# Routing by hand order: exponentials, gates and a cast moved by one step, running counts by TensorE

## The chip, the cores and the metric

The program runs on one core of one Trainium2 chip. The metric is the device time of one execution in microseconds (us); of several runs the median counts. A core has TensorE (PE, with PEld for its weight loads), VectorE (DVE), ScalarE (ACT), GpSimd (POOL), SyncE (SP) and 16 DMA engines. Each engine works through its own list in order; semaphores order the engines among each other.

## The reference

Three layers follow each other over 4608 tokens of 512 numbers: attention within chunks of 64 tokens, a mixture of eight experts with one expert per token, and a dense layer with a maximum over three products.

```python
# attention: 8 batches, 8 heads, 576 tokens in 9 chunks of 64, head size 64
scores = scale * q_c @ k_c.T; scores -= scores.max(-1)
attn = exp(scores); x = (attn / (attn.sum(-1) + 1e-9)) @ v_c
# experts
compute = x @ w_skip > 0                  # the others pass through
logits = x @ w_gate                       # 8 experts
e_idx = argmax(logits)                    # the first of equals
gate = (exp(logits - max) / (sum + 1e-9))[e_idx]
x[compute] += gate * (relu(x @ w1[e_idx]) @ w2[e_idx])
# dense
out = maximum(maximum(x @ m1, x @ m2), x @ m3) @ m_out
```

## The kernel before

The first stage is a software pipeline over 36 tiles of 128 tokens. Step t of its loop (`for t in range(NT + LAG)`) does the scores of tile t, the transposed exponentials of tile t-1 (`trp`), the values of tile t-2 (`xp`, scaled to `xg` by DVE and transposed on PE as `trx`) and the router's logits of tile t-3 (`lp`). Two tiles of tokens make a unit, whose q and k are turned by PE (`trq`, `trk`) one unit ahead. PE's list is in the program's order for the whole loop, the lists of DVE, ACT and POOL up to step 34 (`HAND`); after that a scheduler orders them, and SP's list, which issues the loads, is the scheduler's throughout.

Routing goes by groups of four tiles (the last two groups have two). When the logits of a group's last tile are there (steps 6, 10, 14, ... 30), `route` works out each token's expert: `mx`, `dl`, the exponentials `ex` on ACT (`rex`), the first largest `m8`, the sum `sm`, the gate's reciprocal into a column of the group's rows `xg`, the flag `comp`, and the one-hot row `oh` (`roh` in the trace). `route` is a generator: eight of its pieces (`BY = 8`) run at the end of that step, the others a step later, among them four additions that carry the running count per expert (`run`) from tile to tile. `store_x` sends the group's rows to DRAM by POOL's queue, behind the reciprocal. One step after `route` (7, 11, ... 31), `rank_of` lets PE add up the ranks in one PSUM tile (`rk`): one product of `upper_b` with the one-hot rows and one of `ones_b` with the four running counts. A group's rows lie in one of two buffers, so that group g+2 writes where group g was stored from.

```python
nc.tensor.matmul(rk, upper_b, oh[:, T], start=True, stop=False)                       # L420
link["rank", g] = nc.tensor.matmul(rk, ones_b, before[:, T], start=False, stop=True)  # L421
```

In the same loop expert 0's weights are loaded in eight pieces and split into two parts (`CUTS`, steps 13, 17, 19, 21, 25, 27, 29, 33): the cast `whi_e` on ACT (L93) at the end of the step, and right behind it the remainder `wlo_e` (L94), on POOL at steps 19 and 27 and on DVE otherwise. The router's weights `wcat` are loaded by SP (L607, L608) between the loads of units 2 and 3.

After the loop come the experts (their first products are `h`), and then the dense layer (`f_a`, `f_b`, `f_d`, `o`), whose text is not changed.

Of the kernel before, what the change touches and what calls it, by code (L numbers as in the profile page):

```python
# [34 lines left out]
COLS = NT  # L35
SLOTS = E * COLS
# [4 lines left out]
def kernel(  # L41
# [72 lines left out]
    ew = {}  # L114
# [7 lines left out]
    def expert_piece(e, i, pool, eng=None, raw=None):  # L122
        ew[e, i] = load_split(pool, *expert_src(e, i), eng, raw)
# [3 lines left out]
    kpool = p1.enter_context(tc.tile_pool(name="kpool", bufs=1))  # L127
# [5 lines left out]
    ones_b = kpool.tile([P, P], BF16, name="ones_b")  # L133
# [14 lines left out]
    prio = kpool.tile([P, GT, E], F32, name="prio")  # L148
# [4 lines left out]
    tok_f = kpool.tile([P, NT], F32, name="tok_f")  # L153
    col_i = kpool.tile([P, P], I32, name="col_i")
    col_f = kpool.tile([P, P], F32, name="col_f")
    run = [kpool.tile([P, GT, E], BF16, name=f"run{i}") for i in range(2)]
    nc.scalar.mul(run[0].rearrange("p t e -> p (t e)"), ones_b[:, :GT * E], 0.0)
    ids_sb = cpool.tile([P, SLOTS], I32, name="ids_sb")
    ids_0 = cpool.tile([P, 3], I32, name="ids_0")
    edge = kpool.tile([P, 2], I32, name="edge")  # L160
# [11 lines left out]
    apool = p1.enter_context(tc.tile_pool(name="apool", bufs=2))  # L172
# [182 lines left out]
    def route(g):  # L355
        (parts, lg), nt = groups[g], SIZES[g]
        T = slice(0, nt)

        def small(nm, dt=F32, w=None):
            return apool.tile([P, GT] if w is None else [P, GT, w], dt, tag=nm, name=f"{nm}_{g}", bufs=1)  # L360

        logit, skip = lg[:, T, :E], lg[:, T, E]
        mx = small("rmx")
        yield nc.vector.reduce_max(mx[:, T], logit, axis=AX)
        dl = small("rdl", w=E)
        yield nc.vector.tensor_tensor(dl[:, T], logit, mx[:, T].unsqueeze(2).to_broadcast([P, nt, E]), op=ALU.subtract)
        ex = small("rex", w=E)
        link["routed"] = nc.scalar.activation(ex[:, T], dl[:, T], AF.Exp)
        pr = small("rpr", w=E)
        yield nc.vector.scalar_tensor_tensor(pr[:, T], dl[:, T], 0.0, prio[:, T], op0=ALU.is_ge, op1=ALU.mult)  # L370
        m8 = small("rm8")
        yield nc.vector.reduce_max(m8[:, T], pr[:, T], axis=AX)
        sm = small("rsm")
        yield nc.vector.reduce_sum(sm[:, T], ex[:, T], axis=AX)
        yield nc.vector.tensor_scalar_add(sm[:, T], sm[:, T], 1e-9)
        for i, part in enumerate(parts):
            n = part.shape[1]
            yield nc.vector.reciprocal(part[:, :, DM], sm[:, i * n:i * n + n])
        store_x(g)
        comp = small("rcomp")  # L380
        yield nc.vector.tensor_single_scalar(comp[:, T], skip, 0.0, op=ALU.is_gt)
        m8c = small("rm8c")
        yield nc.vector.tensor_mul(m8c[:, T], m8[:, T], comp[:, T])
        oh = small("roh", BF16, w=E)
        yield nc.vector.tensor_tensor(oh[:, T], prio[:, T], m8c[:, T].unsqueeze(2).to_broadcast([P, nt, E]), op=ALU.is_equal)
        before, after = run[g % 2], run[(g + 1) % 2]
        for j in range(nt):
            last = j == nt - 1
            yield nc.vector.tensor_tensor(
                after[:, 0, :] if last else before[:, j + 1, :], before[:, j, :], oh[:, j, :], op=ALU.add)  # L390
        eo = small("reo")
        yield nc.vector.tensor_scalar(eo[:, T], m8[:, T], float(-COLS), float(E * COLS + P * SLOTS), op0=ALU.mult, op1=ALU.add)
        nc.vector.scalar_tensor_tensor(eo[:, T], comp[:, T], float(-P * SLOTS), eo[:, T], op0=ALU.mult, op1=ALU.add)
        picks[g] = oh, eo

    def advance(gen, by):
        for _ in range(by):
            if next(gen, None) is None:
                return

    def fill_first(have):
        cp = ps_sm("pad_ps")[:, :1]
        nc.tensor.matmul(cp, ones_b, have, start=True, stop=True)
        pad = apool.tile([P, 1], I32, name="pad", bufs=1)
        nc.vector.scalar_tensor_tensor(pad, cp, -1.0, edge[:, 0:1], op0=ALU.mult, op1=ALU.add)
        nc.vector.tensor_tensor(pad, pad, edge[:, 1:2], op=ALU.max)
        nc.vector.tensor_single_scalar(pad, pad, 7, op=ALU.arith_shift_right)
        nc.vector.tensor_tensor(have, have, pad, op=ALU.add)

    def count_first():  # L410
        cp = ps_sm("first_ps")[:, :1]
        nc.tensor.matmul(cp, ones_b, run[0][:, 0, E - 1:E], start=True, stop=True)
        nc.vector.tensor_scalar_add(cnt_i[:, 2 * E:], cp[0:1, :], float(P))

    def rank_of(g):
        oh = picks[g][0]
        before = run[g % 2]
        T, nt = slice(0, SIZES[g]), SIZES[g]
        rk = ps_sm(f"rk{g}")[:, :nt * E].rearrange("p (t e) -> p t e", e=E)
        nc.tensor.matmul(rk, upper_b, oh[:, T], start=True, stop=False)  # L420
        link["rank", g] = nc.tensor.matmul(rk, ones_b, before[:, T], start=False, stop=True)  # L421
        picks["rk", g] = rk

    def rank_out(g):
# [176 lines left out]
    def in_turn(load, *what):  # L601
        with tc.issue_after(link["load"].ins) if "load" in link else nullcontext():
            load(*what)

    first_v = {1: (0, 1), 2: (2, 3), 3: (4, 5), 4: (6, 7)}
    def load_gates():
        nc.sync.dma_start(wcat[:, :, :E], w_gate.rearrange("(c p) e -> p c e", p=P))  # L607
        link["load"] = nc.sync.dma_start(wcat[:, :, E], w_skip.rearrange("(c p) -> p c", p=P))  # L608

    for u in range(5):  # L610
        in_turn(load_qk, u)
        for part in first_v.get(u, ()):
            in_turn(load_v, part)
        if u == 2:
            in_turn(load_gates)
        if u < 2:
            pair_heads(u, 0)
            pair_heads(u, 1)
            if u == 0:
                qk_transpose(0, 0)  # L620
                qk_transpose(0, 1)
    LAG, late, raws_0 = GT + 5, range(NT - 2), {}
    HAND = NT - 2
    CUTS = [13, 17, 19, 21, 25, 27, 29, 33]
    ASIDE = (19, 27)
    BY = 8
    routing = {}
    fetch = None
    in_order = ExitStack()
# [5 lines left out]
    def last_of(t):  # L635
        if 0 <= t < NT:
            g, j = PLACE[t]
            if j + 1 == SIZES[g]:
                return g
        return None  # L640

    for t in range(NT + LAG):
        u, s = divmod(t, 2)
        hand = t < HAND
# [38 lines left out]
            qk_transpose(u + 1, s, "k")  # L683
        if t < NT:
            exponentials(t)
        if 0 <= t - 2 < NT:
            x_transpose(t - 2)
            x_out(t - 2)
        if t < NT:
            cross_up(t)  # L690
        g = last_of(t - 3)
        if g is not None:
            routing[g] = route(g)
            advance(routing[g], BY if hand else 99)
        g = last_of(t - 4)
        if g is not None:
            advance(routing[g], 99)
            rank_of(g)
            if not t + 1 < HAND:
                rank_out(g)  # L700
        g = ranked if hand else last_of(t - 4)
        if g is not None:
            if g == 2:
                count_first()
            place(g)
            if g == FIRST or START[g] + SIZES[g] == DIRECT:
                for i in range(max(late[0], t - LAG + hand), START[g + 1]):
                    send_id(i)
                late = range(START[g + 1], NT - 2)
            if START[g] + SIZES[g] == DIRECT:  # L710
                load_ids(ids_0[:, 2:], ids_rows[:, 2:3])
            if g == FIRST:
                fill_first(run[(g + 1) % 2][:, 0, 0:1])
                load_ids(ids_0[:, :2], ids_rows[:, :2])
                xgs[0] = [four_kb([P, XW], F32, f"xg_0_{j}") for j in range(2)]
                rows = START[g + 1] * P
                fetch = t + 3
        if t in CUTS:
# [500 lines left out]
```

## Time and profile before

| | |
|---|---|
| runs shown | 1122.0 us median of 3 (1117.78, 1122.0, 1122.71) |
| profiled execution | 1125.63 us; span from first to last instruction 1123.9 us |
| TensorE's granted clock, mean over the span | 0.954 |
| busy | PE 1035.0 us (92%), DVE 577.0 (51%), ACT 432.9 (39%), POOL 356.4 (32%) |
| first stage | span up to about 215 us; the first product of expert 0 starts at 223.9 us |

A row of the timeline has the start and the length in us, engine, line, operation, what it writes and reads, and in brackets how long the engine stood idle before it and who released it. Views by tile list the engine's idle time before the tile's instructions, in us and times. Views of windows give busy time and number of instructions per engine, the granted clock (1.00 is full, 0.50 half), the DMA engines' share and GB/s.

### The profile page before, as it was taken

The numbers are of one execution on the slowest core, as the hardware profiler recorded it, in microseconds if no ns is written. First come the engines' busy times: TensorE is split into PE (matmuls) and PEld (weight loads), VectorE is DVE, ScalarE is ACT, GpSimd is POOL, SyncE is SP. The second block draws the span as 40 slices with busy tenths as digits, with TensorE's granted clock in tenths as the row PEclk, the third lists the DMA queues.
The fourth block names the chain that finished last, engine by engine and source line by source line (L and its number), as shares of the span: only waits on it lengthen the run. The fifth ranks groups of instructions, "written<-read, shape, count | busy, mean of one in ns | idle before, by whom it ended". The sixth has DMA issues, their size and how long they took to land.

```text
span 1123.9 us, 19739 instructions
## 1 busy us (share of the span) xinstructions
PE 1035.0 (92%) x7544; PEld 881.6 (78%) x7544; DVE 577.0 (51%) x1116; ACT 432.9 (39%) x771; POOL 356.4 (32%) x379
## 2 busy tenths in 40 slices
PE   7987888897899998999899799999999999999996
PEld 6876777785788887787687688888887888788995
DVE  4566654547873657551479871335234342443241
ACT  5665565433442434441344342222322232223231
POOL 3534554354441335340333141222311140113011
PEclk9898888698999998999999999999999999999998
DMA  9999572246783737471998924664466545666681
GB/s 220 272 271 299 154 196 86 79 153 218 255 285 112 237 109 264 165 229 58 311 298 294 330 87 151 199 193 122 160 193 181 170 140 166 183 185 208 195 263 38
DMA packets 213042, 217.14 MB, mean 193 GB/s; under 512 B 48203, under 2 KB 177227, under 8 KB 212928
## 3 DMA queue, kind: packets, MB, share of 16 engines
q1 hardware_dynamic: 199744, 174.18, 52.0%
q0 software_dynamic: 10592, 33.20, 8.4%
q10 hardware_dynamic: 2592, 8.26, 2.1%
q8 instruction: 70, 1.15, 0.4%
q14 instruction: 44, 0.36, 0.1%
HBM read 175.15 MB, written 41.83 MB: 193 GB/s over the span
## 4 chain that ended last, share of the span: by engine, by line
PE 42%; DMA 5%; issue 3%; POOL 1%; DVE 1%; SPq 0%; ACT 0%; POOLq 0%; DVEq 0%; ACTq 0%
PE f_a L774 5%; PE f_a L775 5%; PE f_a L776 5%; PE o L774 4%; PE o L775 4%; PE o L776 4%; DMA ws<-m_sums 3%; PE f_d L774 3%; PE f_d L776 3%; PE f_d L775 3%; DMA m_sums<-n_q 1%; PE f_b L774 1%; PE f_b L776 1%; PE f_b L775 1%; PE trf L948 1%
## 5 line engine op out<-in xcount | busy, mean ns | idle before, releaser
L94 POOL TENSOR_TENSOR fh<-best,fh 128x512 fp32r<-128x512 f32 (+1 forms) x60 | 76.3, 1278 | 371.9 <-ACT fh L93 286.2
L774 PE MATMUL f_a<-x_t,ws 128*128 128x512 f32 (+1 forms) x270 | 100.3, 372 | 1.0 <-DVE best L1102 1.0
L775 PE MATMUL f_a<-x_t,ws 128*128 128x512 f32 (+1 forms) x270 | 99.7, 369 | 0.0
L776 PE MATMUL f_a<-x_t,ws 128*128 128x512 f32 (+1 forms) x270 | 99.5, 369 | 0.0
L93 ACT CAST whi_e<-raw_e 128x1024 fp32r<-128x1024 f32 x64 | 66.1, 1050 | 59.5 <-DMA raw_e<-in_moe_w_dram 29.8
L774 PE MATMUL h<-xhi,whi_e 128*128 128x256 f32 x256 | 75.6, 296 | 11.9 <-ACT whi_e L93 5.4
L775 PE MATMUL o<-wlo_m,fh 128*128 128x512 f32 x216 | 84.5, 391 | 0.0
L774 PE MATMUL o<-whi_m,fh 128*128 128x512 f32 x216 | 84.2, 392 | 0.0
L776 PE MATMUL o<-whi_m,fh 128*128 128x512 f32 x216 | 83.4, 393 | 0.0
L94 POOL TENSOR_TENSOR wlo_e<-raw_e,whi_e 128x1024 fp32r<-128x1024 f32 x23 | 58.3, 2540 | 53.9 <-ACT whi_e L93 52.6
L775 PE MATMUL h<-xlo,whi_e 128*128 128x256 f32 x256 | 74.7, 292 | 0.1
L776 PE MATMUL y<-whi_e,hlo 128*128 128x512 f32 x184 | 73.0, 400 | 1.7 <-DVE hlo L781 1.4
L774 PE MATMUL y<-whi_e,hhi 128*128 128x512 f32 x184 | 73.9, 403 | 0.6 <-ACT hhi L841 0.6
L776 PE MATMUL h<-xhi,wlo_e 128*128 128x256 f32 x256 | 74.2, 291 | 0.0
L775 PE MATMUL y<-wlo_e,hhi 128*128 128x512 f32 x184 | 72.5, 396 | 0.0
L93 ACT CAST fh<-best 128x512 fp32r<-128x512 f32 (+1 forms) x60 | 34.6, 579 | 94.1 <-DVE best L1104 56.3
L94 DVE TENSOR_TENSOR wlo_e<-raw_e,whi_e 128x1024 fp32r<-128x1024 f32 x41 | 50.8, 1256 | 35.9 <-ACT whi_e L93 34.0
L774 PEld LDWEIGHTS h<-xhi,whi_e 128*128 128x128 f32 x256 | 51.3, 200 | 14.9 <-issue 6.0
L774 PEld LDWEIGHTS f_a<-x_t,ws 128*128 128x128 f32 x270 | 51.1, 189 | 10.1 <-DVE best L1102 1.5
L776 PEld LDWEIGHTS f_a<-x_t,ws 128*128 128x128 f32 x270 | 51.1, 189 | 8.6
L775 PEld LDWEIGHTS f_a<-x_t,ws 128*128 128x128 f32 x270 | 51.1, 189 | 8.4
L765 POOL DMA_INDIRECT x_dram<-xg,ids_sb x20 | 20.5, 1026 | 115.7 <-DVEq L989 46.7
(222 smaller groups left out, 2692.2 us busy)
## 6 DMA issues: line engine op xcount, KB each, us to landing
ws<-m_sums SPq DMA_DIRECT2D x135, 512.0 KB
raw_e<-in_moe_w_dram SPq DMA_DIRECT2D x64, 512.0 KB
ws<-m_sums SPq DMA_DIRECT2D x45, 256.0 KB
x<-x_dram SPq DMA_DIRECT2D x36, 256.0 KB
x_dram<-xg POOLq DMA_DIRECT2D x8, 1040.0 KB
v_all<-in_v_dram SPq DMA_DIRECT2D x32, 256.0 KB
out_dram<-os SPq DMA_DIRECT2D x32, 256.0 KB
m_sums<-n_raw ACTq DMA_DIRECT2D x18, 448.0 KB
```

The costliest lines, as they stand in the source:

```text
L93: nc.scalar.copy(hi, src),
L94: eng.tensor_tensor(lo, src, hi.bitcast(F32), op=ALU.subtract),
L765: ins = nc.gpsimd.indirect_dma_start(out=x_dram[:, :], out_offset=bass.IndirectOffsetOnAxis(ap=ids, axis=0), in_=xg, in_offset=None, bound ...
L774: nc.tensor.matmul(acc, ahi, bhi, start=first, stop=False, skip_group_check=onto)
L775: nc.tensor.matmul(acc, ahi, blo, start=False, stop=False, skip_group_check=onto)
L776: return nc.tensor.matmul(acc, alo, bhi, start=False, stop=last, skip_group_check=onto)
L948: nc.tensor.transpose(tr[:, i * P:(i + 1) * P], row[:, c * P:(c + 1) * P], ident)
```

## The change

- `route` is no longer a generator. In its step it now runs ahead of the transposition `trx` in the program, and it goes as far as `oh`. What is left (the sum, the gate's reciprocal, `eo`, the store, the count) is a new function `gates`, one step later. So ACT's exponentials `rex` have a step until DVE reads them, and the store's issue on POOL stands a step later.
- The running count is kept per group: DVE sums the four one-hot rows (`rgot`) and adds them once. The ranks within a group are added by PE: three more products of `ones_b` with one-hot rows (one in a group of two).
- `CUTS` is one lower, so that load and cast come a step earlier; the remainder stays at the old step.
- `wcat` is loaded by POOL's queue, ahead of its first other transfers.

```diff
         link["routed"] = nc.scalar.activation(ex[:, T], dl[:, T], AF.Exp)
+        comp = small("rcomp")
+        nc.vector.tensor_single_scalar(comp[:, T], skip, 0.0, op=ALU.is_gt)
...
+        m8c = small("rm8c")
+        nc.vector.tensor_mul(m8c[:, T], m8[:, T], comp[:, T])
+        oh = small("roh", BF16, w=E)
+        nc.vector.tensor_tensor(oh[:, T], prio[:, T], m8c[:, T].unsqueeze(2).to_broadcast([P, nt, E]), op=ALU.is_equal)
...
+    def gates(g):
...
+        nc.vector.reduce_sum(sm[:, T], ex[:, T], axis=AX)
+        nc.vector.tensor_scalar(eo[:, T], m8[:, T], float(-COLS), float(E * COLS + P * SLOTS), op0=ALU.mult, op1=ALU.add)
+        nc.vector.tensor_scalar_add(sm[:, T], sm[:, T], 1e-9)
+        nc.vector.scalar_tensor_tensor(eo[:, T], comp[:, T], float(-P * SLOTS), eo[:, T], op0=ALU.mult, op1=ALU.add)
...
+            nc.vector.reciprocal(part[:, :, DM], sm[:, i * n:i * n + n])
         store_x(g)
...
-        for j in range(nt):
-            last = j == nt - 1
-            yield nc.vector.tensor_tensor(
-                after[:, 0, :] if last else before[:, j + 1, :], before[:, j, :], oh[:, j, :], op=ALU.add)
+        nc.vector.reduce_sum(got, oh[:, T].rearrange("p t e -> p e t"), axis=AX)
+        nc.vector.tensor_tensor(after, before, got, op=ALU.add)
...
-        link["rank", g] = nc.tensor.matmul(rk, ones_b, before[:, T], start=False, stop=True)
+        for j in range(nt - 1):
+            nc.tensor.matmul(
+                rk[:, j + 1:], ones_b, oh[:, j:j + 1].to_broadcast([P, nt - 1 - j, E]), start=False, stop=False)
+        link["rank", g] = nc.tensor.matmul(
+            rk, ones_b, before.unsqueeze(1).to_broadcast([P, nt, E]), start=False, stop=True)
...
-        nc.sync.dma_start(wcat[:, :, :E], w_gate.rearrange("(c p) e -> p c e", p=P))
-        link["load"] = nc.sync.dma_start(wcat[:, :, E], w_skip.rearrange("(c p) -> p c", p=P))
+        nc.gpsimd.dma_start(wcat[:, :, :E], w_gate.rearrange("(c p) e -> p c e", p=P))
+        nc.gpsimd.dma_start(wcat[:, :, E], w_skip.rearrange("(c p) -> p c", p=P))
...
-    CUTS = [13, 17, 19, 21, 25, 27, 29, 33]
-    ASIDE = (19, 27)
+    CUTS = [12, 16, 18, 20, 24, 26, 28, 32]
+    ASIDE = (18, 26)
...
+        g = last_of(t - 3)
+        if g is not None and hand:
+            route(g)
         if 0 <= t - 2 < NT:
             x_transpose(t - 2)
...
-            routing[g] = route(g)
-            advance(routing[g], BY if hand else 99)
+        if g is not None and not hand:
+            route(g)
+            gates(g)
         g = last_of(t - 4)
         if g is not None:
-            advance(routing[g], 99)
+            if t <= HAND:
+                gates(g)
             rank_of(g)
...
         if t in CUTS:
             i = CUTS.index(t)
-            expert_piece(0, i, wpool, nc.gpsimd if t in ASIDE else None, raw=raws_0[i])
...
+            nc.scalar.copy(hi_0, raws_0[i])
+            ew[0, i] = hi_0, lo_0
+        if t - 1 in CUTS:
+            i = CUTS.index(t - 1)
+            hi_0, lo_0 = ew[0, i]
+            (nc.gpsimd if t - 1 in ASIDE else nc.vector).tensor_tensor(lo_0, raws_0[i], hi_0.bitcast(F32), op=ALU.subtract)
```

On DVE, at the first group's ranks (step 7), between the shift of the scores (`ex`, from `sc`) and the scaling of the next tile (`sm`), there stood before:

```order
L275 TENSOR_TENSOR ex_825<-sc_806,mx_823 128x2x4x64
L383 TENSOR_TENSOR rm8c_861<-rm_0_769,rcomp_776 128x4
L385 TENSOR_TENSOR roh_863<-prio,rm8c_861 128x32
L389 TENSOR_TENSOR run_114<-run_114,roh_863 128x8 x3
L389 TENSOR_TENSOR run_115<-run_114,roh_863 128x8
L392 TENSOR_SCALAR reo_869<-rm_0_769 128x4
L393 SCALAR_TENSOR_TENSOR reo_869<-rcomp_776,reo_869 128x4
L427 TENSOR_TENSOR rrs_875<-rk_872,roh_863 128x32
L322 TENSOR_SCALAR sm_907<-xp_890 128x8
```

and in the changed kernel, at the same place:

```order
L275 TENSOR_TENSOR ex_827<-sc_808,mx_825 128x2x4x64
L389 TENSOR_REDUCE rsm_863<-rex_757 128x4
L390 TENSOR_SCALAR reo_769<-rm_0_763 128x4
L391 TENSOR_SCALAR rsm_863<-rsm_863 128x4
L392 SCALAR_TENSOR_TENSOR reo_769<-rcomp_759,reo_769 128x4
L395 RECIPROCAL xg_356<-rsm_863 128x4
L399 TENSOR_REDUCE rgot_870<-roh_767 128x8
L400 TENSOR_TENSOR run_115<-run_114,rgot_870 128x8
L432 TENSOR_TENSOR rrs_879<-rk_873,roh_767 128x32
L322 TENSOR_SCALAR sm_911<-xp_894 128x8
```

The one-hot rows `roh`, which PE's ranks read, have left this step; the sum, the reciprocal and the one addition of the count have come in.

On ACT, around the first piece of expert 0's weights (steps 12 and 13), a step running from `aT` to `vm`, there stood before:

```order
L229 COPY vm_1288<-v_all_134 64x260
L292 COPY aT_1442<-trp_1437 128x512
L251 COPY qT_1346<-trq_1_1444 128x2x2x128
L353 COPY lg_1098<-lp_1450 128x9
L251 COPY kT_1359<-trk_1_1456 128x2x2x128
L282 ACTIVATE ex_1435<-ex_1435 128x512
L342 COPY xt_1468<-trx_1463 128x512
L229 COPY vm_1388<-v_all_135 64x260
L93 CAST whi_e_0_1471<-raw_e_0_912 128x1024
L292 COPY aT_1541<-trp_1536 128x512
```

and in the changed kernel:

```order
L229 COPY vm_1294<-v_all_134 64x260
L729 CAST whi_e_0_1389<-raw_e_0_806 128x1024
L292 COPY aT_1451<-trp_1446 128x512
L251 COPY qT_1350<-trq_1_1453 128x2x2x128
L353 COPY lg_1100<-lp_1459 128x9
L251 COPY kT_1363<-trk_1_1465 128x2x2x128
L282 ACTIVATE ex_1444<-ex_1444 128x512
L342 COPY xt_1477<-trx_1472 128x512
L229 COPY vm_1395<-v_all_135 64x260
L292 COPY aT_1545<-trp_1540 128x512
```

The cast has moved ahead by one step of ACT's list, while DVE's remainder `wlo_e` stands behind the same shift of the scores as before.

## Rows read from the trace of the kernel before

**Rows 1.** The page's part 2: TensorE's granted clock in 40 equal slices, tenths.

```profile
PEclk9898888698999998999999999999999999999998
```

**Rows 2.** DVE's line of each step's maxima: ns least/median/most, first and last start.

```profile
L273 DVE TENSOR_REDUCE mx<-sc x36: 679/680/691, 12.1 to 211.6; 128x8 f32<-128x512 f32 x36
```

**Rows 3.** Timeline of PE, two steps next to each other, the scores' first row.

```profile
51.11 0.65 PE L264 MATMUL sc<-kT,qT 64*64 64x64 f32 x32
...
54.95 0.65 PE L264 MATMUL sc<-kT,qT 64*64 64x64 f32 x32
```

**Rows 4.** By tile, `rk`: PE's idle time until a releaser, us, times.

```profile
  DVE run L389: 6.9, 7
  DVE roh L385: 4.8, 5
  ACT ex L282: 2.4, 2
```

**Rows 5.** By tile, `trx`: the same.

```profile
  DVE xg L324: 13.3, 11
```

**Rows 6.** Timeline around one group's ranks, DVE, POOL and PE.

```profile
111.63 0.39 DVE L385 TENSOR_TENSOR roh<-prio,rm8c 128x32 bf16<-128x32 f32 x1
...
112.03 0.61 POOL L235 COPY qr<-qt 128x512 f32<-128x512 f32 x1
112.05 1.55 DVE L389 TENSOR_TENSOR run<-run,roh 128x8 bf16<-128x8 bf16 x4
...
112.08 0.19 PE L420 MATMUL rk<-roh,upper_b 128*128 128x32 bf16 x1 [1.10 <-DVE roh L385]
...
113.46 0.18 PE L421 MATMUL rk<-run,ones_b 128*128 128x32 bf16 x1 [1.19 <-DVE run L389]
```

**Rows 7.** Timeline around one piece of expert 0's weights.

```profile
125.87 1.04 ACT L93 CAST whi_e<-raw_e 128x1024 fp32r<-128x1024 f32 x1
...
126.95 1.22 DVE L94 TENSOR_TENSOR wlo_e<-raw_e,whi_e 128x1024 fp32r<-128x1024 f32 x1 [3.48 <-ACT whi_e L93]
...
128.58 0.69 DVE L324 TENSOR_TENSOR xg<-xp,sm 128x512 f32<-128x512 f32 x1
...
129.41 0.63 PE L337 MATMUL trx<-ident,xg 128*128 128x128 f32 x4 [1.96 <-DVE xg L324]
```

**Rows 8.** Windows: length, busy (x) of PE, PEld, DVE, ACT, POOL, PEclk, DMA share, GB/s.

```profile
28.00:206.00 178.00, 145.37 (x2656) 131.17 (x2655) 104.67 (x314) 110.66 (x227) 87.13 (x140) 0.87 0.75 202
206.00:227.00 21.00, 19.65 (x204) 17.99 (x204) 13.54 (x65) 6.62 (x16) 6.50 (x7) 0.52 0.29 104
20.00:106.00 86.00, 72.47 (x1415) 66.34 (x1409) 51.75 (x149) 56.38 (x118) 40.16 (x72) 0.88 1.06 275
```

**Rows 9.** Timeline of ACT in the first of the two steps of rows 3.

```profile
54.10 0.64 ACT L251 COPY kT<-trk 128x512 f32<-128x512 f32 x1 [0.32 <-PE trk L249]
```

**Rows 10.** Timeline of PE: two rank products of which the second waits for nothing.

```profile
213.77 0.18 PE L420 MATMUL rk<-roh,upper_b 128*128 128x32 bf16 x1 [0.64 <-ACT lg L353]
213.80 0.19 PE L421 MATMUL rk<-run,ones_b 128*128 128x32 bf16 x1
```

**Rows 11.** Timeline: the sum in routing on DVE, and POOL's store with a later write.

```profile
108.52 0.19 DVE L374 TENSOR_REDUCE rsm<-rex 128x4 f32<-128x32 f32 x1 [1.10 <-ACT rex L368]
...
187.06 0.81 POOL L496 DMA_DIRECT2D x_dram<-xg  x1 [9.01 <-DVE sm L322]
...
191.93 0.15 POOL L320 MEMSET xg<- 128x14 f32 x2 [2.35 <-DMA x_dram<-xg]
```

**Rows 12.** Timeline of SP: the first of the two loads of `wcat`.

```profile
15.44 1.53 SPq L607 DMA_DIRECT2D wcat<-in_moe_w_gate_dram  x1
```

**Rows 13.** Waits of PE, 0 to 60 us and 160 to 215 us: total, times, longest.

```profile
PE trp L289 <- issue: 1.8, 1, 1.8
...
PE sc L264 <- issue: 3.9, 8, 1.3
```

**Rows 14.** DVE's line of the running count: ns least/median/most.

```profile
L389 DVE TENSOR_TENSOR run<-run,roh x36: 130/164/603, 44.3 to 231.3; 128x8 bf16<-128x8 bf16 x36
```

More of the change, by code (lines that the diff above doesn't have):

```diff
@@ L155 @@
     col_f = kpool.tile([P, P], F32, name="col_f")
-    run = [kpool.tile([P, GT, E], BF16, name=f"run{i}") for i in range(2)]
-    nc.scalar.mul(run[0].rearrange("p t e -> p (t e)"), ones_b[:, :GT * E], 0.0)
+    run = [kpool.tile([P, E], BF16, name=f"run{i}") for i in range(2)]
+    nc.scalar.mul(run[0], ones_b[:, :E], 0.0)
     ids_sb = cpool.tile([P, SLOTS], I32, name="ids_sb")
@@ L363, in route @@
         mx = small("rmx")
-        yield nc.vector.reduce_max(mx[:, T], logit, axis=AX)
+        nc.vector.reduce_max(mx[:, T], logit, axis=AX)
         dl = small("rdl", w=E)
-        yield nc.vector.tensor_tensor(dl[:, T], logit, mx[:, T].unsqueeze(2).to_broadcast([P, nt, E]), op=ALU.subtract)
+        nc.vector.tensor_tensor(dl[:, T], logit, mx[:, T].unsqueeze(2).to_broadcast([P, nt, E]), op=ALU.subtract)
         ex = small("rex", w=E)
         link["routed"] = nc.scalar.activation(ex[:, T], dl[:, T], AF.Exp)
+        comp = small("rcomp")
@@ L369, in route @@
+        nc.vector.tensor_single_scalar(comp[:, T], skip, 0.0, op=ALU.is_gt)
         pr = small("rpr", w=E)
-        yield nc.vector.scalar_tensor_tensor(pr[:, T], dl[:, T], 0.0, prio[:, T], op0=ALU.is_ge, op1=ALU.mult)
+        nc.vector.scalar_tensor_tensor(pr[:, T], dl[:, T], 0.0, prio[:, T], op0=ALU.is_ge, op1=ALU.mult)
         m8 = small("rm8")
-        yield nc.vector.reduce_max(m8[:, T], pr[:, T], axis=AX)
-        sm = small("rsm")
-        yield nc.vector.reduce_sum(sm[:, T], ex[:, T], axis=AX)
@@ L375, in route @@
-        yield nc.vector.tensor_scalar_add(sm[:, T], sm[:, T], 1e-9)
+        nc.vector.reduce_max(m8[:, T], pr[:, T], axis=AX)
+        m8c = small("rm8c")
+        nc.vector.tensor_mul(m8c[:, T], m8[:, T], comp[:, T])
+        oh = small("roh", BF16, w=E)
+        nc.vector.tensor_tensor(oh[:, T], prio[:, T], m8c[:, T].unsqueeze(2).to_broadcast([P, nt, E]), op=ALU.is_equal)
+        eo = small("reo")
+        picks[g] = oh, eo
+        routing[g] = ex, m8, comp
+    def gates(g):
+        parts, nt = groups[g][0], SIZES[g]
+        T = slice(0, nt)
+        ex, m8, comp = routing[g]
+        oh, eo = picks[g]
+        sm = apool.tile([P, GT], F32, tag="rsm", name=f"rsm_{g}", bufs=1)
+        nc.vector.reduce_sum(sm[:, T], ex[:, T], axis=AX)
+        nc.vector.tensor_scalar(eo[:, T], m8[:, T], float(-COLS), float(E * COLS + P * SLOTS), op0=ALU.mult, op1=ALU.add)
+        nc.vector.tensor_scalar_add(sm[:, T], sm[:, T], 1e-9)
+        nc.vector.scalar_tensor_tensor(eo[:, T], comp[:, T], float(-P * SLOTS), eo[:, T], op0=ALU.mult, op1=ALU.add)
@@ L376, in route @@
         for i, part in enumerate(parts):
             n = part.shape[1]
-            yield nc.vector.reciprocal(part[:, :, DM], sm[:, i * n:i * n + n])
+            nc.vector.reciprocal(part[:, :, DM], sm[:, i * n:i * n + n])
         store_x(g)
[L380 to L385, printed above, removed]
@@ L386, in route @@
-        before, after = run[g % 2], run[(g + 1) % 2]
-        for j in range(nt):
-            last = j == nt - 1
-            yield nc.vector.tensor_tensor(
-                after[:, 0, :] if last else before[:, j + 1, :], before[:, j, :], oh[:, j, :], op=ALU.add)
-        eo = small("reo")
-        yield nc.vector.tensor_scalar(eo[:, T], m8[:, T], float(-COLS), float(E * COLS + P * SLOTS), op0=ALU.mult, op1=ALU.add)
-        nc.vector.scalar_tensor_tensor(eo[:, T], comp[:, T], float(-P * SLOTS), eo[:, T], op0=ALU.mult, op1=ALU.add)
@@ L394, in route @@
[L394 to L399, printed above, removed]
+        before, after = run[g % 2], run[(g + 1) % 2]
+        got = apool.tile([P, E], F32, tag="rgot", name=f"rgot_{g}", bufs=1)
+        nc.vector.reduce_sum(got, oh[:, T].rearrange("p t e -> p e t"), axis=AX)
+        nc.vector.tensor_tensor(after, before, got, op=ALU.add)
     def fill_first(have):
@@ L411, in count_first @@
         cp = ps_sm("first_ps")[:, :1]
-        nc.tensor.matmul(cp, ones_b, run[0][:, 0, E - 1:E], start=True, stop=True)
+        nc.tensor.matmul(cp, ones_b, run[0][:, E - 1:E], start=True, stop=True)
         nc.vector.tensor_scalar_add(cnt_i[:, 2 * E:], cp[0:1, :], float(P))
@@ L614 @@
         if u == 2:
-            in_turn(load_gates)
+            load_gates()
         if u < 2:
@@ L623 @@
     HAND = NT - 2
-    CUTS = [13, 17, 19, 21, 25, 27, 29, 33]
-    ASIDE = (19, 27)
-    BY = 8
+    CUTS = [12, 16, 18, 20, 24, 26, 28, 32]
+    ASIDE = (18, 26)
     routing = {}
@@ L690 @@
             cross_up(t)
-        g = last_of(t - 3)
-        if g is not None:
-            routing[g] = route(g)
-            advance(routing[g], BY if hand else 99)
+        if g is not None and not hand:
+            route(g)
+            gates(g)
         g = last_of(t - 4)
         if g is not None:
-            advance(routing[g], 99)
+            if t <= HAND:
+                gates(g)
             rank_of(g)
@@ L712 @@
             if g == FIRST:
-                fill_first(run[(g + 1) % 2][:, 0, 0:1])
+                fill_first(run[(g + 1) % 2][:, 0:1])
                 load_ids(ids_0[:, :2], ids_rows[:, :2])
@@ L719 @@
             i = CUTS.index(t)
-            expert_piece(0, i, wpool, nc.gpsimd if t in ASIDE else None, raw=raws_0[i])
+            hi_0 = wpool.tile([P, 1024], F32R, tag="w", name=f"whi_e0_{i}")
+            lo_0 = wpool.tile([P, 1024], F32R, tag="w", name=f"wlo_e0_{i}")
+            nc.scalar.copy(hi_0, raws_0[i])
[4 more added lines that the diff above has]
+            (nc.gpsimd if t - 1 in ASIDE else nc.vector).tensor_tensor(lo_0, raws_0[i], hi_0.bitcast(F32), op=ALU.subtract)
+            ew[0, i] = [w.rearrange("p (a b) -> p a b", a=2) if i > 3 else w for w in ew[0, i]]
         if t == fetch:
@@ L730 @@
     cp = ps_sm("cnt_ps")[:, :E]
-    nc.tensor.matmul(cp, ones_b, run[len(SIZES) % 2][:, 0, :], start=True, stop=True)
+    nc.tensor.matmul(cp, ones_b, run[len(SIZES) % 2], start=True, stop=True)
     nc.vector.tensor_copy(cnt_i[:, :E], cp[0:1, :])
```

## The prediction, on record before the changed kernel ran

> **What bounds the kernel now.** I began with the page's slices of the granted clock [rows 1]: in the whole span the low digits lie in the first fifth, one slice at 6. The change touches that part alone, the 36 steps of attention and routing. Next I looked for the stage's beat. DVE's maxima come once a step, 36 times from 12.1 to 211.6 us [rows 2]: 199.5 us in 35 intervals, 5.70 us a step. The PE timeline shows what a step costs when nothing waits: from one step's scores to the next's 3.84 us [rows 3], with PE's work back to back. 35 such intervals would take 134.4 us, so the stage loses 65 us. The rest of this working asks where they are, by the views of the tiles for which PE waits, and then by windows for the clock.
>
> PE waits in two places. Ahead of the rank products it stands 6.9 us for the running count, 4.8 for the one-hot rows and 2.4 where the page names ACT [rows 4]: 14.1 us in the seven groups ranked inside the hand order. Ahead of `trx` it stands 13.3 us for the scaled rows, 11 times [rows 5]. The timelines show why. At the ranks, the one-hot rows are made after the shift of the same step's scores and then come four dependent additions, 1.55 us; PE stands 1.10 us for the first and 1.19 for the second [rows 6]. At a piece of weights, DVE holds its list 3.48 us for ACT's cast, which is ACT's last work of the step; the scaling queued behind comes late, and PE stands 1.96 us [rows 7]. PE's list cannot pass a waiting product, so these 27.4 us lie on the path.
>
> After such stops the granted clock falls. From 28 to 206 us its mean is 0.87 [rows 8]; it has only a full and a half level (2.4 and 1.2 GHz), so 0.13 x 178 = 23.1 us of full-speed work were lost. 14.1 + 13.3 + 23.1 = 50.5 us of the 65; most of the rest are stops marked "issue", 1.8 and 3.9 us in the two places shown [rows 13], which the change doesn't address.
>
> **The change part by part.** All sums go from the profiled execution, 1125.6 us (span 1123.9 and 1.7 around it); the median of the runs is 1122.0, 3.6 less, and I subtract the same amount from it.
>
> *Ranks.* The one-hot rows are now ready a step ahead, the count of the groups before likewise; no operand of the rank products is made in their own step any more. -14.1 us. Later in that step is then only PE itself: 21 more products with their weight loads in the hand order (3 for each of 7 groups). Two rank products that waited for nothing start 0.03 us apart and run 0.19 [rows 10]: between 0.6 (21 x 0.03) and 4.0 us (21 x 0.19); I take 0.1 each, since the weights are loaded anew each time, +2.1.
>
> *Casts.* The remainder stays at its step and the cast stands a step ahead, so the 3.48 us waits of DVE go. The exponentials' sum moves a step too: DVE's 1.10 us for `rex` [rows 11] goes, which also delayed the scaling. -13.3. What is late next is ACT: in a quiet step it idles just 0.32 us [rows 9] against a cast of 1.04 [rows 7], 0.72 us over for each of 8 pieces. The casts are there before as well, so the price lies between 0 and 5.8 us; I take the middle, +3.
>
> *Clock.* Some dips follow the "issue" stops and will stay. Bounds are 0 and 23.1 us; I take about half, -12. The scheduled tail from 206 to 227 us runs at 0.52 [rows 8] and loses 0.48 x 21 = 10.1 us; a stop for a cast precedes it, but there PE also meets routing's last chains. Bounds 0 and 10.1, I take -3.
>
> *Router's weights.* SP is rid of two issues, the first of 1.53 us [rows 12], 3.1 for two like it, just ahead of the loads of unit 3, behind which PE stops 1.8 us [rows 13]. On POOL they stand before its first copies, where it waits for loads anyway; the packets then mix with the very first q and k. Between -3.1 and +3.1; I take half of the gain, -1.5. The Trainium skill (DMA: Bandwidth & Descriptors, Issuing engines are not separate DMA queues) says that all queues share the same 16 DMA engines, so that another issuer saves its issue time alone. The DMA share of 1.06 from 20 to 106 us [rows 8] agrees that those engines are full there; by this rule the term would be nearer 0, and the time 1.5 us longer.
>
> *Store.* The store's issue on POOL stands a step later, behind the reciprocal in `gates`; queued behind it are the next step's index writes and copies of q and k, which have steps to spare (POOL waited 9.01 us to issue the store shown [rows 11]). But the buffer is written again by group g+2, now three steps after the issue, not four. Once in the trace POOL stands 2.35 us for a store, and goes on at 191.93, 4.87 us after that store's issue at 187.06 [rows 11]. Three quiet steps are 11.5 us. Between 0 and 7 x 2.35 = 16.5 us; I take +1.5, near 0, as the space is twice the one landing seen.
>
> *DVE's load.* Eight operations after the shift become seven in the rank step, and eight seven in the step before, each about 0.2 us in a gap that DVE has there; it is busy 104.7 of 178 us [rows 8]. I count 0. The running count took from 0.13 to 0.60 us [rows 14], the long ones beside POOL's copies [rows 6]. Were six operations with two operands in each group (four before the one-hot rows, two in `gates`) held 0.44 us (0.60 - 0.16), 7 groups would cost 18 us of DVE, and the time would be 1103 if all of it reached PE. The Trainium skill (SBUF — State Buffer, SBUF: two separate sides) gives a lock as the reason: a VectorE operation with two operands in SBUF and one of GpSimd exclude each other for the whole instruction. That rule speaks against the four such operations that now stand together; rows 14 agree with it in the range, and rows 6 in the neighbour.
>
> Sum: -14.1 - 13.3 - 12 - 3 - 1.5 + 2.1 + 3 + 1.5 = -37.3. 1125.6 - 37.3 = 1088.3; by the median 1122.0 - 37.3 = 1084.7, so **1085 us**. What follows the stage starts earlier by the same and is otherwise the same text; the scheduler changes some order in the dense layer, for which I count 0.
>
> **Rivals.**
> - *All the clock returns.* With no stop left above a microsecond, the other 11.1 of the stage and 7.1 of the tail come too: 1085 - 18 = 1067. For it: quiet steps run at full clock. Against: the "issue" stops.
> - *The clock stays down.* The waits go, but short ones remain in each cast and rank step and the dips with them: 12 + 3 back, 1100.
> - *Loads bind.* From 20 to 106 us the DMA engines are full at 275 GB/s [rows 8]. By 206 us 43.7 MB pass at most (36.0 from 28 us on at 202 GB/s, 7.7 before at 275). At 275 that takes 159 us, no bound; at 238, halfway between the two rates, 184, so the stage could gain 22 us; with the 6.6 us added, 15: 1107.
> - *DVE binds*, by operations held 18 us beside POOL's: 1103. For it: the range of rows 14. Against: DVE is free two fifths of the stage.
> - *Given back at the seam*, where expert 0 waits for the ids, the gather and the next weights, whatever the stage does: 1120.
> - *Slower, by the store.* A store lands so late that group g+2's scaling waits on DVE and PE behind it, and half a dip follows. Before any loss, 37.3 us must be eaten, 5.6 more to be measured: 6.1 us in each of 7 groups. That is a landing some 18 us after issue (11.5 + 6.1). At 7.5 us each: 1122 + 15 = 1137. For it: full DMA engines early on. Against: the one wait seen ends within 5 us.
>
> **How the numbers follow.** Forecast 0.42, with its own range 1077 to 1094; all the clock 0.13; clock down 0.14; loads 0.12; DVE 0.07; seam 0.05; slower 0.07. The bounds of the terms alone reach from 1122 - 27.4 - 33.2 - 3.1 + 0.6 = 1059 to 1122 - 27.4 + 3.1 + 4.0 + 5.8 + 16.5 = 1124. The range 1066 to 1112 leaves out the seam, the slower case and the ends. A measurement of this kernel tells about 0.5% (5.6 us) from no change: faster 0.88, same 0.05, slower 0.07.
>
> **What would show it.** In the changed profile: no idle time of PE before `rk` released by `roh` or `run`; idle time before `trx` by `xg` under 4 us; DVE not waiting for `whi_e` or `rex` in the hand order; the last of the 36 maxima near 176 us (211.6 less 36); a granted clock of 0.93 or more from 28 us to the end of the steps. POOL or DVE released by `x_dram<-xg` more than once would be the store's price. The prediction is wrong if the beat stays above 5 us with those waits gone, or if the first product of expert 0 comes less than 20 us earlier than 223.9.

## The result, and the profile after

The changed kernel takes 1089.7 us (1087.7 to 1093.9) where the kernel before, run beside it, takes 1120.4: a ratio of 0.973 (95% interval 0.969 to 0.977), 30.8 us less. Forecast were 1085, in a range from 1066 to 1112. The profiled execution has a span of 1092.1 us.

The whole gain lies ahead of expert 0. Its first product starts at 191.8 us instead of 223.9, 32.0 earlier; from there to the end of the span it is 900.3 us, before 900.0. The page's slices of the clock and of the DMA share:

```profile
PEclk9989978989999989998999899999999999999998
DMA  9999684467738185428998545663566546666581
```

Against [rows 1] no slice of the first fifth is under 7. The maxima of the steps, then what PE waits for ahead of `rk` and of `trx` (each by tile: total, times), answering to [rows 2, 4, 5]:

```profile
L273 DVE TENSOR_REDUCE mx<-sc x36: 679/680/692, 12.1 to 179.5; 128x8 f32<-128x512 f32 x36
...
L423 PE MATMUL rk<-roh,ones_b x26: 166/169/182, 39.8 to 199.6; 128*128 128x8 bf16 x10, 128*128 128x24 bf16 x8, 128*128 128x16 bf16 x8
...
  ACT lg L353: 1.3, 1
...
  ACT aT L292: 42.9, 12
  PE lp L348: 0.7, 1
  DVE xg L324: 0.6, 1
```

The last maxima come 32 us earlier; the beat is 4.78 us (167.4 in 35), not 5.70. No rank product waits for DVE any more: the 1.3 us for `lg` belong to a group that is ranked after the last step's scores, at 181.65 us. The scaled rows cost 0.6 us instead of 13.3. But `trx` has a new releaser, ACT's copy `aT`; the tile view adds PE and its weight loads. The waits from 28 to 185 us keep them apart (total, times, longest):

```profile
POOL vm L223 <- DMA v_all<-in_v_dram: 23.4, 6, 9.7
...
PE trx L337 <- ACT aT L292: 20.6, 5, 7.0
...
DVE wlo_e L734 <- ACT whi_e L729: 15.3, 3, 6.7
ACT whi_e L729 <- DMA raw_e<-in_moe_w_dram: 14.3, 4, 5.7
...
ACT vm L229 <- DMA v_all<-in_v_dram: 6.4, 3, 5.3
...
POOL xg L320 <- DMA x_dram<-xg: 4.2, 1, 4.2
```

Two loads are late: expert 0's raw weights and `v`. The second longest stop stands at step 13; here are its rows on SyncE's queue, ACT and PE:

```profile
58.31 2.60 SPq L100 DMA_DIRECT2D raw_e<-in_moe_w_dram  x1
...
60.75 0.41 ACT L229 COPY vm<-v_all 64x260 f32<-64x260 f32 x1
66.88 1.04 ACT L729 CAST whi_e<-raw_e 128x1024 fp32r<-128x1024 f32 x1 [5.73 <-DMA raw_e<-in_moe_w_dram]
67.83 0.58 ACT L292 COPY aT<-trp 128x512 f32<-128x512 f32 x1
...
68.47 0.90 PE L337 MATMUL trx<-ident,xg 128*128 128x128 f32 x3 [5.70 <-ACT aT L292]
```

ACT's list cannot pass the cast, and the next step's `aT` stands behind it. The load is asked for in the code five steps ahead, at step 7, whose scores start at 36.54 us. But SyncE's list runs far behind the code: it issues the load at 58.31, in step 12 itself, 2.9 us before ACT is free for the cast (60.75 + 0.41). At step 29 the same happens with `v`, first on ACT, then PE stands 7.0 us:

```profile
149.65 0.41 ACT L229 COPY vm<-v_all 64x260 f32<-64x260 f32 x1 [5.25 <-DMA v_all<-in_v_dram]
151.82 1.04 ACT L729 CAST whi_e<-raw_e 128x1024 fp32r<-128x1024 f32 x1 [1.76 <-DMA raw_e<-in_moe_w_dram]
152.78 0.58 ACT L292 COPY aT<-trp 128x512 f32<-128x512 f32 x1
```

What stands ahead of these loads on SyncE's queue is a run of 32 small ones (L204, 64 KB each, one head of q or k), from 107.78 us to 144.47, with other loads in between; its beginning:

```profile
107.78 3.67 SPq L204 DMA_DIRECT2D qt<-in_q_dram  x4
111.55 1.41 SPq L204 DMA_DIRECT2D kt<-in_k_dram  x2
113.07 0.65 SPq L216 DMA_DIRECT2D v_all<-in_v_dram  x1
113.81 1.42 SPq L100 DMA_DIRECT2D raw_e<-in_moe_w_dram  x1
115.28 1.20 SPq L204 DMA_DIRECT2D kt<-in_k_dram  x2
```

Over these 36.7 us the DMA engines have a share of 0.63 at 185 GB/s; from 28 us up to there it is 1.09 at 283 (columns as in [rows 8]):

```profile
107.78:144.47 36.69, 32.24 (x697) 29.83 (x696) 25.39 (x83) 26.60 (x56) 20.09 (x29) 0.87 0.63 185
28.00:107.78 79.78, 69.65 (x1521) 64.60 (x1519) 56.60 (x169) 61.23 (x128) 51.70 (x81) 0.95 1.09 283
```

The windows (columns as in [rows 8]) from 28 us to the last step's scores, before and then after, and the stretch up to expert 0 after:

```profile
28.00:208.60 180.60, 147.36 (x2696) 132.86 (x2699) 106.48 (x317) 111.35 (x229) 87.13 (x140) 0.86 0.75 202
```

```profile
28.00:176.20 148.20, 125.91 (x2709) 116.40 (x2711) 101.03 (x302) 108.16 (x226) 88.49 (x137) 0.91 0.93 243
176.20:191.80 15.60, 13.10 (x167) 11.98 (x158) 9.35 (x48) 5.84 (x15) 7.79 (x9) 0.68 0.29 105
```

The stretch is 32.4 us shorter. PE's idle time in it (length less busy) fell from 33.2 to 22.3 us, 10.9; its busy time for the same products from 147.4 to 125.9, 21.5. Of the latter the clock explains most: added up over the trace, the clock stood at the lower level for 50.5 us before, 3.4 of them while PE stood still, and for 27.3 after, 11.1 of them in stops. Work at half speed fell from 47.1 to 16.2 us, worth 15.4. Some 6 us of busy time I cannot assign; the ends of products are modelled.

Step by step the trace shows where the lower clock lies. Before, it came in the step behind each stop at the ranks: 2.8, 3.1, 7.1, 2.6 and 2.5 us of it in steps 8, 12, 16, 20 and 24. In the changed kernel these five steps have none, and all of the 27.3 us lie in the steps with the new stops, 13, 21, 27 and 29, and the step behind each.

The stretch from the last step's scores to expert 0 became no shorter: 15.3 us before (208.55 to 223.88, all of it at the lower level) and 15.6 after. PE works 1.6 us less in it and stands 1.9 us more.

### The profile page after: what moved, and what is told of

Its sections match the earlier page's. It is cut to its first block, busy times and chain, and to the rows that moved or that the text cites. A ratio compares the mean times of both kernels' runs of the same rounds, so it can differ in the third digit from the quotient of the medians.

```text
span 1092.1 us, 19781 instructions
## 1 busy us (share of the span) xinstructions
PE 1015.1 (93%) x7570; PEld 867.2 (79%) x7570; DVE 570.8 (52%) x1100; ACT 431.2 (39%) x771; POOL 359.6 (33%) x381
## 2 busy tenths in 40 slices
DMA packets 212050, 217.14 MB, mean 199 GB/s; under 512 B 47195, under 2 KB 176235, under 8 KB 211936
## 3 DMA queue, kind: packets, MB, share of 16 engines
q8 instruction: 70, 1.15, 0.4%
## 4 chain that ended last, share of the span: by engine, by line
PE 46%; DMA 5%; issue 1%; DVE 1%; POOL 1%; ACT 0%; SPq 0%; POOLq 0%; DVEq 0%; ACTq 0%
PE f_a L789 6%; PE f_a L791 6%; PE f_a L790 6%; PE o L789 5%; PE o L791 4%; PE o L790 4%; PE f_d L789 3%; PE f_d L790 3%; PE f_d L791 3%; DMA ws<-m_sums 3%; PE f_b L789 1%; PE f_b L791 1%; PE f_b L790 1%; DMA m_sums<-n_q 1%; PE trf L963 1%
## 5 line engine op out<-in xcount | busy, mean ns | idle before, releaser
L93 ACT CAST whi_e<-raw_e 128x1024 fp32r<-128x1024 f32 x56 | 57.7, 1050 | 67.0 <-DMA raw_e<-in_moe_w_dram 35.6
L94 POOL TENSOR_TENSOR wlo_e<-raw_e,whi_e 128x1024 fp32r<-128x1024 f32 x21 | 53.0, 2531 | 57.0 <-ACT whi_e L93 55.7
L789 PEld LDWEIGHTS h<-xhi,whi_e 128*128 128x128 f32 x256 | 51.1, 199 | 16.3 <-ACTq L1066 10.2
L1122 ACT COPY p<-f_a 128x512 f32<-128x512 f32 (+1 forms) x45 | 24.4, 545 | 90.8 <-PE f_a L791 90.6
L780 POOL DMA_INDIRECT x_dram<-xg,ids_sb x20 | 20.8, 1041 | 112.9 <-DVEq L1004 46.8
```

The source lines that it names most:

```text
L93: nc.scalar.copy(hi, src),
L94: eng.tensor_tensor(lo, src, hi.bitcast(F32), op=ALU.subtract),
L780: ins = nc.gpsimd.indirect_dma_start(out=x_dram[:, :], out_offset=bass.IndirectOffsetOnAxis(ap=ids, axis=0), in_=xg, in_offset=None, bound ...
L789: nc.tensor.matmul(acc, ahi, bhi, start=first, stop=False, skip_group_check=onto)
L1122: nc.scalar.copy(p1, acc_a)
```

## The experiments

Each set has its own runs of the kernel before beside it (medians from 1118 to 1127 us), so ratios are compared, not times. One profile alone tells little below 6 us: the changed kernel, profiled again (e5), starts expert 0 at 197.9 us instead of 191.8, after waits of other sizes, and its ratio is the same.

**Theories.** A: each wait removed is worth its length, as the prediction's sum has it. B: the loads' bytes bind from some 20 us on. C: ACT itself is late, its cast longer than its slack.

**e1, the casts back.** The changed kernel with

```
-    CUTS = [12, 16, 18, 20, 24, 26, 28, 32]
+    CUTS = [13, 17, 19, 21, 25, 27, 29, 33]
...
-            nc.scalar.copy(hi_0, raws_0[i])
...
+            expert_piece(0, i, wpool, nc.gpsimd if t in ASIDE else None, raw=raws_0[i])
```

> The changed kernel with the two casts of expert 0's weights back where they stood (first and second cast in one step, at 13, 17, 19, 21, 25, 27, 29, 33); ranks, gates and the weights' queue stay changed. Theory A (the sum's term): the casts' move is worth 13.3 of waits less 3 for ACT, so this runs 10 to 16 us slower than the changed kernel's 1089.7, at 1100 to 1106, and trx waits for xg about 13 us again. Theory B (the loads bind in the middle of the steps): the steps lost at the casts are mostly given back by waits for loads that go, so it runs 0 to 5 us slower, 1090 to 1095: the waits of ACT's first cast for its raw weights (14.3 us in 4) shrink to under 4 while trx waits for xg.

0.983 (0.979 to 0.987), 1104.6 us. With the changed kernel at 0.973 and, later, 0.974 the casts' move is worth 10 to 11 us on top of the rest, the number of A. A's reason is not shown by it: `trx` waits for `xg` 8.6 us in 6, not 13, and PE's idle time from 28 us to the last maxima is 20.2 us here, against 23.3 and 17.9 in the two profiles of the changed kernel. Work at half speed is 34.5 us here, 16.2 and 28.0 there.

**e2, the casts alone**: the kernel before with the change's casts and nothing else.

> The kernel before with the casts' move alone. Theory A: 10.3 us of waits and some 4 of the clock go: 1104 to 1110 of 1120.4. Theory B: the beat of the steps stays slow at the ranks (5.7 us a step), so the loads are in time here and the casts are worth their 10 to 14 too (1106 to 1110), and what binds only binds when both moves are made: the two moves done singly add up to more than the 30.8 us done together. A third reading (ACT's cast is what stops aT, whatever the loads): the casts alone gain under 5, over 1115.

0.996 (0.992 to 0.999), 1117.6 us: the third reading's number, not its reason, since PE does not stand for `aT` ahead of `trx` here. The waits of `rk` for `run` grew, from 6.9 to 11.0 us. The longest running count (by tile: least, median, most), DVE's three counts of step 19 and POOL at that time:

```profile
L389 DVE TENSOR_TENSOR run<-run,roh x34: 130/164/2278, 43.2 to 215.0; 128x8 bf16<-128x8 bf16 x34
```

```profile
104.87 3.03 DVE L389 TENSOR_TENSOR run<-run,roh 128x8 bf16<-128x8 bf16 x3
```

```profile
105.34 2.34 POOL L727 TENSOR_TENSOR wlo_e<-raw_e,whi_e 128x1024 fp32r<-128x1024 f32 x1
```

One count of 128x8 elements took 2.28 us, from 105.42 to 107.70; GpSimd's second cast ended at 107.69. The same pair met at step 27, where the count took 2.28 us too. The Trainium skill (SBUF — State Buffer, SBUF: two separate sides) says that a VectorE operation with two operands in SBUF and a GpSimd one that reads it shut each other out for the whole instruction; here the trace agrees, for both counts end 0.02 us after the cast. (Theory F.)

**e11, the casts alone, GpSimd's elsewhere.** As e2 with one line (the remainder is made in the step after the one that `ASIDE` names), which moves GpSimd's two second casts from steps 19 and 27, where ranks are counted, to 17 and 25:

```
-    ASIDE = (18, 26)
+    ASIDE = (16, 24)
```

> The kernel before with the casts' move alone, and GpSimd's two second casts at steps 17 and 25 instead of 19 and 27 (VectorE makes those of 19 and 27 after the step's counts). Theory F (a running count of VectorE that meets GpSimd's cast is held until the cast ends, and so the casts' move alone lost at steps 19 and 27 what it gained): both steps fall from 9.9 and 9.7 us to about 7.3, rk's waits for run from 11.0 to about 7, and the time is 3 to 7 us under the casts alone: 1111 to 1115 where the kernel before has 1124.9, ratio 0.989 to 0.993. Without F: within 2 us, 0.994 to 0.998.

0.982 (0.979 to 0.986): F holds, and is worth 15 us by the two ratios, not 3 to 7. The longest count is 0.60 us again, and steps 19 and 27 take 7.6 us instead of 9.9 and 9.7, 4.4 together. Most of the rest is the clock: from 28 us to the last step 58.0 us stood at the lower level in e2, 34.1 here, and the work done at it fell from 53.5 to 29.8 us, worth 11.8. In e2 the whole 15.4 us of steps 20 and 21 ran at the lower level, in e11 2.5 us of them. So two stops of 3.3 us instead of 1.2 cost several times what they are longer.

So the casts alone give 20 us (e11, with GpSimd's share moved), ranks, gates and queue without them 19 (e1), and both 30: the two moves overlap by some 9 us. Something else binds when both are made.

**e3, the gates' weights back on SyncE's queue.**

```
-        nc.gpsimd.dma_start(wcat[:, :, :E], ...
+        nc.sync.dma_start(wcat[:, :, :E], ...
...
```

> The changed kernel with the gates' weights back on SyncE's queue at their old place. The sum's term: 1.5 us slower (+-3.1), 1088 to 1093, from the first loads of q and k that stand behind them; the rule that the issuing engine makes no difference: within 0.5 us of 1089.7. Theory B expects no difference either, since the first 28 us are bound by bytes (DMA share 1.00).

0.976 (0.972 to 0.981) against 0.973 to 0.974: not told apart.

**e4, one raw load for all eight pieces.**

```
+            if i == 0:
...
                 raws_0[i] = load_raw(*expert_src(0, i))
+            else:
+                raws_0[i] = raws_0[0]
```

> Leaves out seven of the eight loads of expert 0's weights in the steps (3.67 MB): all eight pieces are cast from the first piece's raw weights, so the output is not the reference's. Theory B (loads bind, and a late raw load holds the first cast, aT behind it and trx): the 20.6 us of trx waiting for aT fall under 4, steps 21, 27 and 29 (8.3, 9.5, 11.9 us) run at 4 to 5, the clock stays high, and the time is 1068 to 1078. Theory C (ACT itself is late: a cast of 1.04 against 0.32 of slack in a step): the waits for aT stay at 5 or more, in all eight cast steps, and the time is within 5 us of 1089.7.

0.974 (0.970 to 0.978), as if nothing had been taken away: B falls in the form given. C gave the time, but not the waits: `trx` stands 12.1 us for `aT` in four places, not in all eight cast steps, and the stop at step 21 is gone. ACT stands 10.2 us for `v` (7.9 at step 29), with 3.67 MB fewer to load, and the DMA engines' share from 107.8 to 144.5 us is 0.59. New theory D: SyncE's list holds `v` back, by the 32 small loads of the last two units.

**e5 to e8, four kernels on one chip**: the changed kernel again (e5); the casts later (e6); the small loads by batch (e7); both (e8).

```
-        if t + 5 in CUTS:
+        if t + 7 in CUTS:
...
-    CUTS = [12, 16, 18, 20, 24, 26, 28, 32]
-    ASIDE = (18, 26)
+    CUTS = [14, 18, 21, 24, 28, 30, 32, 33]
+    ASIDE = (18, 30)
```

```
-            for h in range(H):
...
-                        dst[:, h, :], src[b0:b0 + nb, h, WHOLE:, :].rearrange("b (p r) d -> b p (r d)", r=2))
+            for b in range(nb):
+                rows_b = slice(b * TAIL // 2, (b + 1) * TAIL // 2)
...
+                        dst[rows_b], src[b0 + b, :, WHOLE:, :].rearrange("h (p r) d -> p h (r d)", r=2))
```

> The changed kernel itself, as the measure for the others of this set. All theories: 0.973 of the kernel before (0.969 to 0.977), and the stops of TensorE at steps 13, 21, 27 and 29 again, 3 to 7 us each.

> The changed kernel with expert 0's raw weights asked for seven steps ahead of the cast instead of five, and the casts spread later: 14, 18, 21, 24, 28, 30, 32, 33 (POOL's share at 18 and 30). Theory E (ACT's first cast waits for a raw load that SyncE's queue brings late, and holds aT behind it): the stops at steps 13 and 21 (5.7 and 3.1 us, with some 3 us of the lower clock) go, those where v is late (step 29) stay: 5 to 10 us faster than the changed kernel. Theory C (ACT's time itself): no change within 3 us, stops of about the same size at the new cast steps.

> The changed kernel with the last two units of q and k loaded in 16 issues of 128 KB (by batch, 32 partitions each) instead of 32 issues of 64 KB (by head). Theory D (SyncE's queue in order: the 32 issues stand from 107.8 to 144.5 us and hold the v loads behind them): 16 issues at about 0.6 us fewer bring the v loads some 10 us forward, the waits of POOL's and ACT's vm for v (9.7 and 5.3 us) fall under 3, step 29 runs in under 6 us instead of 11.9, and the time is 6 to 12 us under the changed kernel's. Theory B (bytes bind): the same bytes, within 3 us of the changed kernel.

> The two edits together: casts later with raws asked for seven steps ahead, and the last q and k loads in 16 issues. If theories D and E both hold, the stops of TensorE between 28 us and the end of the steps fall from some 24 us to under 8 and the time is 12 to 20 us under the changed kernel's, 0.955 to 0.963 of the kernel before. If the bytes bind (theory B), 0 to 5 us.

Measured 0.974 (0.972 to 0.977), 0.974 (0.971 to 0.977), 0.965 (0.963 to 0.968) and 0.963 (0.960 to 0.967). E falls as a gain: the stops for raw weights at steps 13 and 21 go in e6, and the time stays. D holds, 9.5 us. e8 was expected at 12 to 20 us under the changed kernel and is 11.6 under it; in its trace `trx` waits for `aT` 0.2 us and `v` holds POOL 1.5 at most, yet it is not told apart from e7. e5's expectation missed too: there steps 13 and 21 hardly waited, 27 and 29 did. Why early stops count so little shows in the first scores of step 30, in the changed kernel, e6 (27 of the 32, before a short stop) and e7:

```profile
155.37 1.08 PE L264 MATMUL sc<-kT,qT 64*64 64x64 f32 x32
```

```profile
155.57 1.06 PE L264 MATMUL sc<-kT,qT 64*64 64x64 f32 x27
```

```profile
147.76 0.65 PE L265 MATMUL sc<-kT,qT 64*64 64x64 f32 x32
```

With the 32 small loads in front, step 30 begins at 155.4 (changed), 155.2 (e5), 155.6 (e6) and 157.2 us (e1, which makes its casts otherwise); in e4, with seven loads fewer on SyncE's queue, at 150.7. Most of what is gained before waits there for `v`. In e7 SyncE's 16 issues let `v` pass, and step 29 takes 4.3 us instead of 11.9. The packets are nearly the same (212,178 against 212,050 in the whole program), but from 107.78 to 144.47 us the DMA engines' share is 1.15 at 251 GB/s, not 0.63 at 185. In e7's waits from 28 to 185 us `v` now holds POOL 2.8 us at most, and what is left is the raw weights:

```profile
PE trx L338 <- ACT aT L293: 11.9, 4, 4.9
...
ACT whi_e L730 <- DMA raw_e<-in_moe_w_dram: 10.1, 2, 5.7
...
POOL vm L224 <- DMA v_all<-in_v_dram: 8.1, 4, 2.8
```

**e9, raw weights by GpSimd's queue** (e7's edit and `eng=nc.gpsimd` in their load), and **e10, asked for seven steps ahead** (e7's edit and `t + 7` alone), on one chip; **e12** is e10 once more on another.

> The changed kernel with the last q and k loads in 16 issues and expert 0's raw weights asked for by GpSimd's queue instead of SyncE's, five steps ahead of the cast as they were. If the raw loads are late because they stand in SyncE's list behind q, k and v (theory D), ACT's first cast no longer waits for them (10.1 us in 2 with the 16 issues alone, under 2 here), the stops at steps 13 and 21 (4.4 and 4.9 us) go, and the time is 5 to 10 us under that run's 0.965 of the kernel before: 0.956 to 0.961. If what they wait for is bytes (theory B), v comes late instead and it stays at 0.962 to 0.968.

> The changed kernel with the last q and k loads in 16 issues and the raw weights asked for by SyncE seven steps ahead instead of five, casts where the change put them. Theory D: the stops at steps 13 and 21 shrink to under 2 us each, the v loads come up to 2 us later each time, 3 to 8 us under 0.965 of the kernel before: 0.958 to 0.962. Theory B: 0.963 to 0.968.

> The last run of the set before once more (16 issues for the last q and k, raw weights asked for seven steps ahead): the steps' products ended earliest there (first product of expert 0 at 180.5 us against 191.8), though its ratio was 0.968. If the trace speaks for the time, 0.957 to 0.965 of the kernel before, under the changed kernel's 0.973; if the 16 issues alone are all, 0.965.

0.966 (0.962 to 0.970), 0.968 (0.965 to 0.972) and 0.961 (0.958 to 0.964). The stops at 13 and 21 go in both kernels, but e9 and e10 came out where theory B had them: POOL now stands 27.3 and 19.6 us for `v`, against 8.1 in e7. The traces end their steps earliest of all (first product of expert 0 at 185.2, 180.5 and 182.3 us against 189.9 in e7), but the ratios of e9 and e10 are no better than e7's, and those of the two sets of e10 differ by as much as was sought; the profiled run of e10 is the fastest of its six. e12, 1079.7 us, beats the changed kernel's interval; that it beats e7 is not shown. Its waits and window:

```profile
POOL vm L224 <- DMA v_all<-in_v_dram: 23.2, 9, 4.7
...
ACT vm L230 <- DMA v_all<-in_v_dram: 11.0, 8, 3.2
...
PE trx L338 <- ACT aT L293: 3.8, 4, 2.1
```

```profile
28.00:166.60 138.60, 124.47 (x2709) 114.82 (x2707) 101.72 (x302) 108.25 (x226) 88.46 (x140) 0.96 1.05 259
```

Over the steps as a whole the DMA engines are now full (1.05; 1.00 in e7 to its last step at 174.5 us, 0.93 in the changed kernel, where they were full up to 107.8 us only). By that share the bytes bind here, and a further gain in the steps would have to load less; no run tried it.

## Why the prediction was right, and where its steps were off

- **Ranks, right.** No wait by `roh` or `run` is left. The 21 products cost less than the 2.1 us taken: a step with ranks takes 3.96 us (scores at 36.54 and 40.50), a quiet one 3.84, so 0.12 in each of 7.
- **Casts: the removed wait right (13.3 to 0.6), the price of what is late next mis-sized.** The prediction put ACT's lateness between 0 and 5.8 us, from its time alone, and took 3. PE waits 20.6 us for `aT` in the steps. DVE's waits for the cast, which the prediction saw gone, are 15.3 us in 3 after 24.0 in 6. The cast had been ACT's last work of its step; a step earlier its load, issued behind SyncE's backlog, is not there. The working asked how long the cast takes, not whether its data come; "of a step that is moved, what does it read and when does that land" was the missing line, and the view that shows it is SyncE's timeline, where raw loads and their casts could have been set side by side.
- **Clock, right in its cause, mis-sized the other way in the steps.** Taken were 12 us in the stage; less work at half speed was worth 15.4, and it went where stops went. The forecast of a granted clock of 0.93 or more was missed (0.91 to the last step), but 11.1 of the 27.3 us at the lower level lie in stops, where they cost nothing; the mean of a window cannot show that. For the tail 3 us were taken and none came: the granted clock from the last step's scores to expert 0 rose from 0.50 to 0.68, but the stretch takes 15.6 us instead of 15.3. The window of [rows 8], 206 to 227 us, reaches beyond this stretch at both ends.
- **Router's weights.** -1.5 with bounds of 3.1 either way; e3 cannot tell it from nothing, nor the rule of the shared engines from the gain.
- **Store, right to be near 0.** One wait of POOL for `x_dram`, 4.2 us; PE never stood for it, where 1.5 us were taken.
- **DVE, right at 0.** The operations now made together take at most 0.56 us and stand in gaps. The lock weighed there is real; it costs where PE waits for the held operation, as in e2, and the changed kernel has no such count on DVE beside GpSimd's cast.
- **Seam, right.** 900.0 and 900.3 us.

The sum came out because errors cancel, and that is luck. The terms of waits and added work come to 20.8 us (14.1 + 13.3 less 2.1, 3 and 1.5) and PE's idle time fell by only 10.9, since the stops that came new (20.6 instead of 3) took back more than the casts' 13.3; nothing came of the tail's 3. Against that, PE's busy time in the steps fell by 21.5 where 12 were taken for the clock: 15.4 by the clock and 6 unassigned. Of the rivals, *loads bind* named the resource but not the way: its 1107 took a rate of 238 GB/s as the bound, and the steps ran at 243: at 283 with the engines full up to 107.8 us, then at 185 with a share of 0.63. What held `v` from there on was the order of SyncE's list (e4 against e7); over the steps as a whole the DMA engines were full only once that was mended (e7, e12).

Open are the stops marked "issue", which differ between runs of one kernel (0.6 us before the scores in the changed kernel's profile, 5.2 in e5's), why e10's two sets differ, and how the 30.8 us divide between the moves: e1 and e11 give the sizes, not the reasons.

## What to carry to other kernels

When an operation is moved earlier, look up when the load that it reads is issued, not only where the code asks for it: a queue in order that runs steps behind the code turns "five steps ahead" into none, and whatever stands behind the moved operation on its engine waits too. Count the issues in front of a late load before counting bytes, and look at the DMA engines' share in that stretch; 16 fewer small ones were worth 9.5 us here, seven loads of 512 KB fewer nothing. A stop is worth more than its length where the clock falls after it (e2 against e11: 4.4 us of steps, 15 us of time), so a short wait removed at the right place can pay more than a long one.

## What the hardware showed that I had not expected

- A VectorE addition of 128x8 elements was held 2.28 us (median 0.16) by a GpSimd cast that started 0.08 us earlier, and ended 0.02 us after it.
- Loads of 64 KB held SyncE's queue about as long as loads of 256 KB: 0.5 to 0.7 us each at the shortest, with the engines' share at 0.63, so 32 issues for 2 MB took 37 us with what stood between them.
- The same program shows its stops elsewhere in another set of runs: the changed kernel stood 5.7 us at step 13 in one profile and 0.4 in another, and began step 30 at 155.4 and 155.2 us in both.
